# Linear attention and an ELU MLP on one core: a new start, 64x64 tiles for K^T V, a redistributed ELU and a new order around group 2

## The chip, the cores and the metric

The kernel runs on one core of a Trainium2 chip. The metric is the time of one execution on the device in microseconds (us). Each run also comes with its mean granted TensorE clock (1.0 is full speed).

Engine names: PE is TensorE's matmul, PEld its weight load, DVE VectorE, ACT ScalarE, POOL GpSimd, SP the queue that issues most stores and DMA transposes.

## The reference

```python
kv  = einsum('bhsd,bhse->bhde', k, v)            # per head: K^T V, 64 x 64
out = einsum('bhsd,bhde->bhse', q, kv)           # the "product"
x   = out / sqrt(mean(out*out, -1) + 1e-6) * g_norm
# heads side by side: x is [4608, 512]
h   = x @ w_in                                   # first layer, 512 -> 2048
g   = where(h > 0, h, exp(min(h, 0)) - 1)        # ELU
y   = g @ w_out                                  # second layer, 2048 -> 512
```

q, k and v are 8 batches x 8 heads x 576 rows x 64. The kernel works in nine groups of 512 tokens (512 rows of each batch; group 8 holds the 64 rows left over of each). A group needs 64 first-layer and 64 second-layer matmuls of 128x512, in bf16. While PE works on the MLP of group T, the attention of group T+1 is woven in.

## The kernel before

The start, for group 0: V lands, then twice, for each half of the heads, the same serial chain.

```python
def heads_half(u, se_ps, mean_ps, fill):
    kv_single(0, kv_ps, u)                       # K^T V, 36 matmuls of 64x64
    nc.vector.tensor_copy(out=kv0[:, u], in_=kv_ps[...])
    idle(fill[0])                                # idle matmuls
    ...                                          # product: 4 matmuls into se_ps
    for l in range(2): nc.scalar.activation(sq[l], se_ps[l], AF.Square)
    idle(fill[1])
    ...                                          # mean by a matmul
    for l in range(2):
        nc.scalar.activation(r[l], mean[:, l, :], AF.Ln, bias=eps_col)
        nc.scalar.activation(r[l], r[l], AF.Exp, scale=-0.5)
    for l in range(2): nc.vector.scalar_tensor_tensor(out=x0[...], ...)   # scale
heads_half(0, ..., (1, 3, 0)); heads_half(1, ..., (0, 0, 0))
```

K^T V of the groups from 2 on is computed two heads at a time, 128 wide (half of the result is thrown away), and the weights' side needs both heads side by side, so POOL first copies K into that layout:

```python
for j in range(9):
    for s in range(2):
        nc.tensor.matmul(kv_ps[s][:, u*128:u*128+128],
            lhsT=k_bf[rows, j, 2*u:2*u+2, :], rhs=v[rows, j, 2*u:2*u+2, :], ...)
def unpack(name, b, eng): ...                    # 3 copies of K, 4 of Q, on POOL
```

A "step" i of a group is 8 first-layer matmuls into one of two PSUM pairs, followed by the ELU: Exp on ACT, then min and subtract 1 (a tensor-scalar) and a max with the PSUM pair on DVE. In some steps (`relu`) ACT copies the positive part out of PSUM too, so that DVE no longer reads PSUM and has less work. The order around group 2:

```python
for i in range(2): elu(0, i, [(0, 2, firsts[i])], False)()
for i in range(2, 8): mm1(0, i, relu=i in (2, 4, 6), spare=i in (2, 5))()
...
# group 1; se0, se1: the two halves of group 2's product; x0, x1: its transposes
group(1, at, {"kv": 2, "se0": 4, "se1": 6}, {}, (1, 3, 5, 6), 1)
ahead["qd"]()                                    # DMA transpose of a later Q
mm2_quarter(1, 0, 0); mm2_quarter(1, 0, 1); at["x0"]()   # a quarter: 4 matmuls
mm2_quarter(1, 0, 2); at["x1"](); mm2_quarter(1, 0, 3)
```

The product's PSUM tile exists once: the next product or transpose can start only when DVE has scaled the rows of the one before.

## Time and profile before

| | before |
|---|---|
| time, median of 3 runs | 305.54 us (305.16 to 306.78) |
| span of the profiled run | 304.3 us |
| PE busy | 281.5 us (93%) |
| DVE, ACT, POOL busy | 56%, 47%, 21% |
| mean granted clock | 0.982 |

From the page of the kernel before: busy time by engine, then two rows of the view in 40 equal slices of 7.6 us (busy tenths of PE, tenths of the granted clock).

```profile
PE 281.5 (93%) x1760; PEld 136.1 (45%) x1789; DVE 170.1 (56%) x207; ACT 142.7 (47%) x201; POOL 63.9 (21%) x96
...
PE   7559989886698999999999999999999999999995
...
PEclk9769999999999999999999999999999999999999
```

PE is the bottleneck from slice 14 on, without gaps. In the first three slices it is a quarter to a half idle and its clock is down; slices 9 to 13 have gaps, the largest in 10 and 11. The windows view of the kernel before gives the same by stage. Columns: from:to, length, busy time and number of instructions of each engine, then clock, DMA share, GB/s.

```profile
0.00:25.19 25.19, 16.85 (x131) 6.96 (x134) 7.39 (x15) 10.98 (x17) 12.16 (x22) 0.80 1.07 190
25.19:37.82 12.63, 11.84 (x81) 5.43 (x80) 9.43 (x15) 10.89 (x15) 5.51 (x9) 1.00 1.24 206
37.82:51.81 13.99, 13.02 (x151) 7.22 (x153) 6.95 (x7) 6.14 (x11) 5.55 (x9) 1.00 1.27 188
51.81:83.38 31.57, 24.88 (x172) 12.84 (x173) 18.31 (x22) 18.59 (x26) 17.18 (x24) 1.00 1.20 172
83.38:110.97 27.59, 26.34 (x161) 12.75 (x164) 19.64 (x21) 13.34 (x19) 7.57 (x12) 1.00 0.88 140
110.97:304.30 193.33, 188.62 (x1071) 90.90 (x1087) 108.39 (x127) 82.80 (x116) 15.93 (x23) 1.00 0.41 86
```

The stages end with: group 0's first 16 first-layer matmuls; its other 48; the start of group 1's first layer; of group 2's; of group 3's. The start, in the PE timeline of the kernel before (start, length, what, count, idle time before and its releaser):

```profile
10.41 0.69 PE L191 MATMUL at<-v_pk,k_pk 64*64 64x64 bf16 x36 [2.02 <-DMA v_pk<-in_v_dram]
...
13.94 0.48 PE L191 MATMUL at<-v_pk,k_pk 64*64 64x64 bf16 x36
17.67 0.64 PE L559 MATMUL se_ps<-qT,kv 64*64 64x512 bf16 x4 [3.25 <-DVE kv L554]
...
20.29 5.07 PE L607 MATMUL h_ps<-xT,w_in_sb 128*128 128x512 bf16 x15 [0.22 <-issue]
```

The second half's K^T V is done at 14.4 us, but its product waits until 17.7 us for a copy that stands behind two scalings in DVE's queue. The 16 first matmuls take 4.9 us at the slow clock; at the fast one 16 take 3.45 us. The waits of PE between 51 and 111 us, in the waits view of the kernel before (total us, times, longest):

```profile
PE at L329 <- DVE xs L256: 2.4, 1, 2.4
PE h_ps L407 <- DVE gT L436: 2.1, 3, 0.7
PE at L222 <- DVE xs L256: 1.8, 2, 1.5
PE o_ps L452 <- ACT o_sb L462: 0.7, 1, 0.7
PE at L329 <- ACT xT L336: 0.3, 1, 0.3
```

Line 329 is the transpose of group 2's rows, 222 a product, 407 the first layer, 452 the second.

### The profile page before, as it was taken

Reading aid. Unit: us, or ns where it says so; the run is one execution under the profiler, and the core shown is the slowest. Engines: PE = TensorE matmul, PEld = TensorE weight load, DVE = VectorE, ACT = ScalarE, POOL = GpSimd, SP = SyncE. Lnnn points to the kernel's source line nnn. Section 1 sums busy time; section 2 is a strip of 40 time slices with the busy share of each in tenths; the row PEclk is TensorE's granted clock in tenths of the full one; section 3 lists DMA queues with packets and bytes.
Section 4 is the critical chain, followed back from the end, with each engine's and each line's share of the span. In section 5 each row is a group of like instructions: output and inputs, shape, how many; then the busy total and the mean of one; then the engine's idle time right before and its main releaser. Section 6 shows DMA issues by size and latency. Waiting matters only on the chain.

```text
span 304.3 us, 4381 instructions
## 1 busy us (share of the span) xinstructions
PE 281.5 (93%) x1760; PEld 136.1 (45%) x1789; DVE 170.1 (56%) x207; ACT 142.7 (47%) x201; POOL 63.9 (21%) x96
## 2 busy tenths in 40 slices
PE   7559989886698999999999999999999999999995
PEld 3213445443354445444544444454444444444444
DVE  5036745268539855765577547755774775554400
ACT  3466842578345544543553365345534554333311
POOL 8424309370944004500700000001100000000000
PEclk9769999999999999999999999999999999999999
DMA  7999999999799839696831313154715031101132
GB/s 180 184 206 203 206 203 189 177 214 155 118 182 125 176 88 150 80 175 117 133 103 34 105 35 104 37 124 107 151 34 139 2 103 34 71 0 69 50 91 69
DMA packets 56052, 35.94 MB, mean 118 GB/s; under 512 B 32864, under 2 KB 53600, under 8 KB 56032
## 3 DMA queue, kind: packets, MB, share of 16 engines
q0 software_dynamic: 20128, 17.30, 38.8%
q1 hardware_dynamic: 35504, 17.83, 26.7%
q10 hardware_dynamic: 400, 0.52, 0.5%
q8 instruction: 14, 0.23, 0.3%
q14 instruction: 6, 0.05, 0.1%
HBM read 36.70 MB, written 9.44 MB: 152 GB/s over the span
## 4 chain that ended last, share of the span: by engine, by line
PE 82%; DVE 8%; ACT 5%; DMA 3%; issue 2%; POOL 0%; DVEq 0%; POOLq 0%
PE h_ps L407 36%; PE o_ps L452 33%; PE o_ps L719 5%; DVE gT L436 3%; DMA v_pk<-in_v_dram 3%; ACT elu_e L419 2%; DVE elu_e L428 2%; PE at L177 2%; PE at L222 2%; PE h_ps L607 2%; DVE xs L256 1%; DVE ss L246 1%; PE at L329 1%; PE at L191 1%; DVE xT L338 1%
## 5 line engine op out<-in xcount | busy, mean ns | idle before, releaser
L407 PE MATMUL h_ps<-xT,w_in_sb 128*128 128x512 bf16 (+1 forms) x563 | 131.6, 376 | 3.4 <-DVE gT L436 2.9
L452 PE MATMUL o_ps<-w_out_sb,gT 128*128 128x512 bf16 x491 | 118.4, 379 | 1.8 <-ACT o_sb L462 0.7
L419 ACT ACTIVATE elu_e<-h_ps 128x1024 bf16<-128x1024 f32 (+1 forms) x74 | 73.8, 1004 | 90.9 <-PE h_ps L407 88.7
L407 PEld LDWEIGHTS <-w_in_sb 128*128 128x128 bf16 x568 | 54.2, 98 | 65.4 <-issue 4.8
L436 DVE TENSOR_TENSOR gT<-elu_e,h_ps 128x1024 bf16<-128x1024 bf16 (+1 forms) x66 | 79.5, 1205 | 6.9
L428 DVE TENSOR_SCALAR elu_e<-elu_e 128x1024 bf16<-128x1024 bf16 (+1 forms) x73 | 35.0, 479 | 76.1 <-ACT elu_e L419 75.8
L452 PEld LDWEIGHTS <-gT 128*128 128x128 bf16 x512 | 49.8, 98 | 60.0 <-issue 1.0
L462 ACT COPY o_sb<-o_ps 128x512 f32<-128x512 f32 x32 | 18.7, 586 | 20.8 <-PE o_ps L452 20.8
L246 DVE TENSOR_REDUCE ss<-sq 128x16 f32<-128x1024 bf16 x16 | 19.4, 1218 | 9.0 <-ACT sq L241 8.9
L152 POOL COPY q_bf<-q_pk 128x512 bf16<-128x512 bf16 x24 | 14.2, 637 | 25.2 <-DMA q_pk<-in_q_dram 13.0
L256 DVE TENSOR_TENSOR xs<-at,ss 128x1024 bf16<-128x1024 f32 x15 | 18.2, 1217 | 0.0
L121 POOL DMA_DIRECT2D v_pk<-in_v_dram x10 | 7.4, 740 | 48.0 <-PE at L177 44.9
L241 ACT ACTIVATE sq<-at 128x1024 bf16<-128x1024 f32 x15 | 15.4, 1026 | 3.5 <-PE at L222 3.5
L152 POOL CAST q_bf<-st_q 128x512 bf16<-128x512 f32 x4 | 2.6, 654 | 64.5 <-DMA st_q<-in_q_dram 64.5
L152 POOL COPY k_bf<-k_pk 128x768 bf16<-128x768 bf16 x18 | 15.1, 875 | 2.4 <-DMA k_pk<-in_k_dram 2.4
L719 PE MATMUL o_ps<-w_out_sb,gT 128*128 128x512 bf16 (+1 forms) x79 | 14.0, 336 | 0.1
L107 POOL DMA_DIRECT2D q_pk<-in_q_dram x14 | 10.4, 746 | 3.5 <-DMA v_pk<-in_v_dram 2.0
L719 PEld LDWEIGHTS <-gT 128*128 128x128 bf16 x80 | 7.8, 98 | 6.2
L222 PE MATMUL at<-bd_kv,qT 128*128 128x128 bf16 x104 | 7.9, 219 | 2.7 <-DVE xs L256 1.8
L222 PEld LDWEIGHTS <-qT 128*128 128x128 bf16 x112 | 7.3, 98 | 5.9 <-issue 3.1
L121 POOL DMA_DIRECT2D k_pk<-in_k_dram x10 | 7.5, 751 | 6.3 <-DMA w_in_sb<-in_moe_w_in_dram 2.8
L276 ACT CAST bd_kv<-at 64x256 bf16<-64x256 f32 x12 | 4.4, 367 | 8.3 <-PE at L177 8.2
(60 smaller groups left out, 113.0 us busy)
## 6 DMA issues: line engine op xcount, KB each, us to landing
out_dram<-o_sb SPq DMA_DIRECT2D x16, 512.0 KB, 2.9
q_pk<-in_q_dram POOLq DMA_DIRECT2D x14, 256.0 KB, 4.9
k_pk<-in_k_dram POOLq DMA_DIRECT2D x6, 576.0 KB, 9.8
v_pk<-in_v_dram POOLq DMA_DIRECT2D x6, 576.0 KB, 11.0
w_in_sb<-in_moe_w_in_dram POOLq DMA_DIRECT2D x4, 512.0 KB, 14.7
w_out_sb<-in_moe_w_out_dram POOLq DMA_DIRECT2D x4, 512.0 KB, 15.0
k_pk<-in_k_dram POOLq DMA_DIRECT2D x4, 288.0 KB, 11.7
v_pk<-in_v_dram POOLq DMA_DIRECT2D x4, 288.0 KB, 11.5
```

What stands on the lines that cost most here:

```text
L152: eng.tensor_copy(out=out_, in_=in_)
L222: nc.tensor.matmul(ov[:, u, :, s, :], lhsT=qT(p, j), rhs=bd_kv[:, T, p, :], start=True, stop=True,)
L241: nc.scalar.activation(sq, se_ps, AF.Square)
L246: nc.vector.reduce_sum(out=ss, in_=sq.rearrange("p c (h e) -> p (c h) e", h=H), axis=AX.X)
L256: nc.vector.tensor_tensor(out=xs.rearrange("p c (h e) -> p (c h) e", h=H), in0=se_ps.rearrange("p c (h e) -> p (c h) e", h=H), in1=ss.to_b ...
L407: nc.tensor.matmul(h_ps[a][:, cs], lhsT=w_in_sb[:, c, f * P : f * P + P], rhs=x(c, cs), start=(c == 0), stop=(c == KC - 1),)
L419: nc.scalar.activation(e[:, lo:hi, :], ps, AF.Exp)
L428: nc.vector.tensor_scalar(out=e[:, lo:hi, :], in0=e[:, lo:hi, :], scalar1=1.0, scalar2=1.0, op0=ALU.min, op1=ALU.subtract,)
L436: nc.vector.tensor_tensor(out=gT[T][:, 2 * i + lo : 2 * i + hi, :], in0=e[:, lo:hi, :], in1=h, op=ALU.add if relu else ALU.max,)
L452: nc.tensor.matmul(o_ps[T, j], lhsT=gT[T][:, f, j * P : j * P + P], rhs=w_out_sb[:, f, :], start=(f == 0), stop=(f == FC - 1),)
L462: nc.scalar.copy(o_sb[T][:, j % 2, :], o_ps.pop((T, j)))
L719: nc.tensor.matmul(ps, lhsT=gT[B][:, f, j * P : j * P + P], rhs=w_out_sb[:, f, cols], start=(f == 0), stop=(f == FC - 1),)
```

## The change

Its intent: shorten the start and keep the clock up, take work from PE (tiles) and POOL (K's copies), relieve DVE in group 0, and cover the waits before group 2 with second-layer matmuls of group 1. The core of the diff, with cuts marked:

```diff
# 1. start: halves interleaved, squares split, fillers on PE
-    heads_half(0, [...], lambda: idle_ps, (1, 3, 0))
-    heads_half(1, se_b, ..., (0, 0, 0))
+    kv_first(0); idle(idle_b, 1); se_first(0)
+    square_first(0, A); square_first(1, V)          # V: copy, then multiply
+    idle(idle_b, 3); mean_first(0); idle(idle_b, 1); mean_first(1)
+    log_first(0); exp_first(0); log_first(1)
+    kv_first(1); idle(idle_b, 1); se_first(1); scale_first(0)
+    square_first(2, A); exp_first(1); square_first(3, V); scale_first(1)
+    idle(..., 3); mean_first(2); log_first(2); exp_first(2); idle(..., 1)
+    mean_first(3); log_first(3); exp_first(3); scale_first(2); scale_first(3)
# 2. g_norm: two loads of 64 single numbers -> one row, turned by a matmul with [[1.0]]
# 3. ELU of group 0, and loads of w_out, q2, k2, v2 issued later (cut)
-    for i in range(2): elu(0, i, [(0, 2, firsts[i])], False)()
+    elu(0, 0, [(0, 2, firsts[0])], True, V)()
+    elu(0, 1, [(0, 2, firsts[1])], False, V)()
     for i in range(2, 8):
-        mm1(0, i, relu=i in (2, 4, 6), spare=i in (2, 5))()
+        mm1(0, i, relu=i in (2, 4, 6), spare=i in (2, 5), eng=Q if i in (3, 5) else V)()
# 4., 5. K^T V: kv_mm and K's unpack on POOL removed
+        def kv_all():
+            if T < B:
+                for u in range(2): kv_half(u)()     # 72 matmuls of 64x64
# 6. order around group 2
-    for j in (2, 3, 0, 1): mm2_quarter(0, j, 3)
+    for j in (2, 3): mm2_quarter(0, j, 3)
-    group(1, at, {"kv": 2, "se0": 4, "se1": 6}, {}, (1, 3, 5, 6), 1)
-    ahead["qd"](); ...                              # quarters between x0 and x1
+    ahead["qd"]()
+    second = {2: [(0, 0, 12, 16)], 3: [(0, 1, 12, 16)]}
+    group(1, at, {"kv": 2, "se0": 5, "se1": 7}, second, (1, 3, 5, 7), 1)
+    # and at its end: for j in range(2): mm2(T, j, 0, FC); at[f"x{j}"]()
-    group 2: 12 quarters of group 1's second layer, 1 and 2 per step in turn
+    group 2: 8 quarters, 1 per step
```

The numbers are those of the prediction's points.

More of the change, by code (lines that the diff above doesn't have):

```diff
@@ L123, in fetch_packed_kv, with unpack_q @@
         )
-    def unpack(name, b, eng):
-        t = raw.pop((name, b))
-        if name == "q":
-            bf["q", b] = qkvp.tile([P, J, H, D], BF16, name="q_bf", tag="q")
-            parts = [slice(j, j + 1) for j in range(J)]
-        else:
-            bf["k", b] = qkvp.tile([P, RK, 4, D], BF16, name="k_bf", tag="k")
-            parts = [slice(j, j + 3) for j in range(0, RK, 3)]
-        for js in parts:
-            copy_on(eng, bf[name, b][:, js].rearrange("p j h d -> p h j d"), t[:, :, js])
+    def unpack_q(b, eng):
+        t = raw.pop(("q", b))
+        bf["q", b] = qkvp.tile([P, J, H, D], BF16, name="q_bf", tag="q")
+        for j in range(J):
+            copy_on(eng, bf["q", b][:, j], t[:, :, j])
     def load_w_in(s):
@@ L170, in at_tile @@
         return full if dtype == FP32 else full.bitcast(BF16)
-    def kv_mm(T, kv_ps, u):
-        for j in range(RK):
-            for s in range(2):
-                rows = slice(s * 64, s * 64 + 64)
-                nc.tensor.matmul(
-                    kv_ps[s][:, u * P : u * P + P],
-                    lhsT=bf["k", T][rows, j, 2 * u : 2 * u + 2, :],
-                    rhs=bf["v", T][rows, j, 2 * u : 2 * u + 2, :],
-                    start=(j == 0),
-                    stop=(j == RK - 1),
-                )
     def kv_single(T, kv_ps, u):
@@ L264, in attention @@
         st = {}
-        def kv():
-            if T == B:
-                return
-            kv_ps = at_tile(FP32)
-            for u in range(2):
-                kv_mm(T, [kv_ps[:, 0:512], kv_ps[:, 512:1024]], u)
-            kv_v = kv_ps.rearrange("p (s x e) -> p s x e", s=2, e=P)[:, :, 0:2, :]
-            bd_v = bd_kv[:, T].rearrange("p (s u) e -> p s u e", s=2)
-            for l in range(2):
-                ls = slice(l * 64, l * 64 + 64)
-                nc.scalar.copy(bd_v[ls, :, :, ls], kv_v[ls, :, :, ls])
         def q_t():
@@ L359, in x_dma @@
             return turn, scale
+        def kv_all():
+            if T < B:
+                for u in range(2):
+                    kv_half(u)()
         def kv_half(u):
@@ L375, in kv_half @@
             return product
-        pieces = {"kv": kv, "q": q_t, "qd": q_dma}
+        pieces = {"kv": kv_all, "q": q_t, "qd": q_dma}
         for h in range(2):
@@ L389, with mm1 @@
     gT = {}
-    def mm1(T, i, cols=(slice(0, 512),), relu=False, spare=False):
+    def mm1(T, i, cols=(slice(0, 512),), relu=False, spare=False, eng=nc.vector):
         if i == 0:
@@ L413, in mm1, with elu @@
                     )
-        return elu(T, i, parts, relu)
-    def elu(T, i, parts, relu):
+        return elu(T, i, parts, relu, eng)
+    def elu(T, i, parts, relu, eng):
         e = mlpt.tile([P, 2, G], BF16, name="elu_e", tag="elu_e")
@@ L427, in rest @@
             for lo, hi, h in parts:
-                nc.vector.tensor_scalar(
+                eng.tensor_scalar(
                     out=e[:, lo:hi, :],
@@ L489 @@
     for u in range(2):
-        for name in "kv":
-            fetch_packed_kv(name, 0, slice(2 * u, 2 * u + 2))
-    make_identity(nc, ident)
+        fetch_packed_kv("k", 0, slice(2 * u, 2 * u + 2))
+        if u == 1:
+            make_identity(nc, ident)
+        fetch_packed_kv("v", 0, slice(2 * u, 2 * u + 2))
     for s in range(4):
@@ L496 @@
     packed_kv(1)
-    for u in range(2):
-        for name in "kv":
-            fetch_packed_kv(name, 1, slice(2 * u, 2 * u + 2))
-        load_w_out(u)
-    for s in range(2, 4):
-        load_w_out(s)
-    fetch_packed_q(2)
-    packed_kv(2)
     for name in "kv":
-        fetch_packed_kv(name, 2)
+        fetch_packed_kv(name, 1, slice(0, 2))
+    load_w_out(0)
+    for name in "kv":
+        fetch_packed_kv(name, 1, slice(2, 4))
     zeros = const.tile([P, 512], BF16, name="zeros")
@@ L513 @@
         nc.vector.memset(means[s * 64 : s * 64 + 64, s * 64 : s * 64 + 64], 1.0 / D)
+    one = const.tile([1, 1], FP32, name="one")
+    nc.vector.memset(one, 1.0)
     nc.vector.memset(bd_kv, 0.0)
     fetch_q(0)
-    g_src = bass.AP(tensor=g_norm.tensor, offset=g_norm.offset, ap=[[1, 64], [1, 1]])
-    for i in range(2):
-        nc.sync.dma_start(out=g_col[i * 64 : i * 64 + 64, :], in_=g_src)
+    g_row = const.tile([1, 2, D], FP32, name="g_row")
+    nc.sync.dma_start(
+        out=g_row,
+        in_=bass.AP(tensor=g_norm.tensor, offset=g_norm.offset, ap=[[1, 1], [0, 2], [1, 64]]),
+    )
     q_st = q_tile(0)
@@ L526, with idle @@
     ]
-    idle_ps = ps_m1.tile([P, 2, G], FP32, name="idle_ps", tag="mm1")
-    def idle(n):
+    def idle(ps, n):
         for _ in range(n):
-            nc.tensor.matmul(
-                idle_ps[:, 0, :], lhsT=zeros[:, 0:P], rhs=zeros, start=True, stop=True
-            )
-    idle(9)
+            nc.tensor.matmul(ps, lhsT=zeros[:, 0:P], rhs=zeros, start=True, stop=True)
+    idle_a = ps_m1.tile([P, 2, G], FP32, name="idle_ps", tag="mm1")
+    idle(idle_a[:, 0, :], 9)
     qT0 = attp.tile([P, NPAIR, G], BF16, name="qT", tag="qT")
@@ L543 @@
             nc.vector.tensor_copy(out=qT0[:, 0:2, :], in_=qt_ps[0])
-        idle(2)
+            idle(idle_a[:, 0, :], 2)
     nc.scalar.copy(qT0[:, 2:4, :], qt_ps[1])
+    nc.tensor.matmul(
+        idle_a[:, 1, 0:1],
+        lhsT=g_row.rearrange("p l d -> p (l d)"),
+        rhs=one,
+        start=True,
+        stop=True,
+    )
+    nc.vector.tensor_copy(out=g_col, in_=idle_a[:, 1, 0:1])
+    idle(idle_a[:, 0, :], 6)
     kv_ps = at_tile(FP32).rearrange("p (s x) -> p s x", s=2)
@@ L550, with kv_first, se_first @@
     xT[0] = lambda c, cs: x0[:, c, cs]
-    def heads_half(u, se_ps, mean_ps, fill):
+    sq0 = [attp.tile([P, G], BF16, name="sq0", tag="sq0", bufs=4) for _ in range(KC)]
+    r0 = [attp.tile([P, G], FP32, name="r0", tag="r0", bufs=4) for _ in range(KC)]
+    se0, mean0 = {}, {}
+    def kv_first(u):
         kv_single(0, kv_ps, u)
         nc.vector.tensor_copy(out=kv0[:, u], in_=kv_ps[:, :, u * 64 : u * 64 + 64])
-        idle(fill[0])
+    def se_first(u):
         for l in range(2):
@@ L559, in heads_half @@
                 nc.tensor.matmul(
-                    se_ps[l][s * 64 : s * 64 + 64, :],
+                    se0[2 * u + l][s * 64 : s * 64 + 64, :],
                     lhsT=kv0[ls, u, s, :],
@@ L565, in heads_half @@
                 )
-        sq, r = [], []
-        for l in range(2):
-            sq.append(attp.tile([P, G], BF16, name="sq0", tag="sq0", bufs=4))
-            nc.scalar.activation(sq[l], se_ps[l], AF.Square)
-        idle(fill[1])
-        mean = mean_ps()
-        for l in range(2):
-            nc.tensor.matmul(mean[:, l, :], lhsT=means, rhs=sq[l], start=True, stop=True)
-            if l == 0:
-                idle(fill[2])
-        for l in range(2):
-            r.append(attp.tile([P, G], FP32, name="r0", tag="r0", bufs=4))
-            nc.scalar.activation(r[l], mean[:, l, :], AF.Ln, bias=eps_col)
-            nc.scalar.activation(r[l], r[l], AF.Exp, scale=-0.5)
@@ L580, in heads_half @@
-        for l in range(2):
-            nc.vector.scalar_tensor_tensor(
-                out=x0[:, 2 * u + l, :],
-                in0=se_ps[l],
-                scalar=g_col,
-                in1=r[l],
-                op0=ALU.mult,
-                op1=ALU.mult,
-            )
-    se_a = ps_m1.tile([P, 2, G], FP32, name="se_ps", tag="mm1")
-    heads_half(0, [se_a[:, 0, :], se_a[:, 1, :]], lambda: idle_ps, (1, 3, 0))
-    se_b = [ps_m2.tile([P, DM], FP32, name="se_ps", tag="mm2") for _ in range(2)]
@@ L593, with square_first @@
-    heads_half(
-        1, se_b, lambda: at_tile(FP32).rearrange("p (c f) -> p c f", c=2), (0, 0, 0)
-    )
-    for l in range(2):
-        ls = slice(l * 64, l * 64 + 64)
-        nc.gpsimd.tensor_copy(
-            out=bd_kv[ls, 0].rearrange("p (s u) e -> p u s e", s=2)[:, :, :, ls], in_=kv0[ls]
-        )
+    def square_first(c, eng):
+        if eng is A:
+            nc.scalar.activation(sq0[c], se0[c], AF.Square)
+        else:
+            nc.vector.tensor_copy(out=r0[c], in_=se0[c])
+            nc.vector.tensor_tensor(out=sq0[c], in0=r0[c], in1=se0[c], op=ALU.mult)
@@ new lines, in mean_first, with log_first, exp_first, scale_first @@
+    def mean_first(c):
+        nc.tensor.matmul(mean0[c], lhsT=means, rhs=sq0[c], start=True, stop=True)
+    def log_first(c):
+        nc.scalar.activation(r0[c], mean0[c], AF.Ln, bias=eps_col)
+    def exp_first(c):
+        nc.scalar.activation(r0[c], r0[c], AF.Exp, scale=-0.5)
+    def scale_first(c):
+        nc.vector.scalar_tensor_tensor(
+            out=x0[:, c, :], in0=se0[c], scalar=g_col, in1=r0[c], op0=ALU.mult, op1=ALU.mult
+        )
+    mean_a = ps_m1.tile([P, 2, G], FP32, name="mean_ps", tag="mm1")
@@ new lines @@
+    se_a = ps_m1.tile([P, 2, G], FP32, name="se_ps", tag="mm1")
+    idle_b = ps_m2.tile([P, DM], FP32, name="idle_ps", tag="mm2")
+    for c in range(2):
+        se0[c], mean0[c] = se_a[:, c, :], mean_a[:, c, :]
+    kv_first(0)
+    idle(idle_b, 1)
+    se_first(0)
+    square_first(0, A)
+    square_first(1, V)
+    idle(idle_b, 3)
+    mean_first(0)
+    idle(idle_b, 1)
+    mean_first(1)
+    log_first(0)
+    exp_first(0)
+    log_first(1)
+    kv_first(1)
+    idle(idle_b, 1)
+    for c in range(2, 4):
+        se0[c] = ps_m2.tile([P, DM], FP32, name="se_ps", tag="mm2")
@@ new lines @@
+    se_first(1)
+    scale_first(0)
+    square_first(2, A)
+    exp_first(1)
+    square_first(3, V)
+    scale_first(1)
+    firsts = [ps_m1.tile([P, 2, G], FP32, name="h_ps", tag="mm1") for _ in range(2)]
+    mean_b = at_tile(FP32).rearrange("p (c f) -> p c f", c=2)
+    for c in range(2, 4):
+        mean0[c] = mean_b[:, c - 2, :]
+    idle(firsts[0][:, 0, :], 3)
+    mean_first(2)
+    log_first(2)
+    exp_first(2)
+    idle(firsts[0][:, 0, :], 1)
+    mean_first(3)
+    log_first(3)
+    exp_first(3)
@@ L602 @@
+    scale_first(2)
+    scale_first(3)
     gT[0] = mlpg.tile([P, FC, G], BF16, name="gT", tag="gT")
@@ L613 @@
                 )
-    for i in range(2):
-        elu(0, i, [(0, 2, firsts[i])], False)()
     at, ahead = attention(1), attention(2)
+    elu(0, 0, [(0, 2, firsts[0])], True, V)()
+    elu(0, 1, [(0, 2, firsts[1])], False, V)()
     for i in range(2, 8):
-        mm1(0, i, relu=i in (2, 4, 6), spare=i in (2, 5))()
+        mm1(0, i, relu=i in (2, 4, 6), spare=i in (2, 5), eng=Q if i in (3, 5) else V)()
+        if i == 2:
+            for l in range(2):
+                ls = slice(l * 64, l * 64 + 64)
+                nc.gpsimd.tensor_copy(
+                    out=bd_kv[ls, 0].rearrange("p (s u) e -> p u s e", s=2)[:, :, :, ls],
+                    in_=kv0[ls],
+                )
+        if i in (3, 5):
+            load_w_out(i // 2)
         if i == 5:
             at["q"]()
+    load_w_out(3)
+    fetch_packed_q(2)
+    packed_kv(2)
+    for name in "kv":
+        fetch_packed_kv(name, 2)
     at["kv0"]()
@@ L643 @@
     at["x1"]()
-    unpack("q", 2, Q)
-    unpack("k", 2, Q)
+    unpack_q(2, Q)
     ahead["qd"]()
     rest = mm1(1, 0, (slice(0, 256), slice(256, 512)))
-    for j in (2, 3, 0, 1):
+    for j in (2, 3):
         mm2_quarter(0, j, 3)
@@ L657, in fetch @@
                 fetch_packed_kv(name, b)
-            unpack("q", b, Q)
-            unpack("k", b, Q)
+            unpack_q(b, Q)
         else:
@@ L676, in group @@
                     at[name]()
+                for j in range(2):
+                    mm2(T, j, 0, FC)
+                    at[f"x{j}"]()
                 break
@@ L688 @@
     at, ahead = ahead, attention(3)
-    group(1, at, {"kv": 2, "se0": 4, "se1": 6}, {}, (1, 3, 5, 6), 1)
     ahead["qd"]()
-    mm2_quarter(1, 0, 0)
-    mm2_quarter(1, 0, 1)
-    at["x0"]()
-    mm2_quarter(1, 0, 2)
-    at["x1"]()
-    mm2_quarter(1, 0, 3)
+    second = {2: [(0, 0, 12, 16)], 3: [(0, 1, 12, 16)]}
+    group(1, at, {"kv": 2, "se0": 5, "se1": 7}, second, (1, 3, 5, 7), 1)
     for T in range(2, NT):
@@ L700 @@
         if T == 2:
-            quarters = [(1, j, 4 * i, 4 * i + 4) for j in range(1, J) for i in range(4)]
-            second = {i: [quarters.pop(0) for _ in range(1 + i % 2)] for i in range(8)}
+            second = {i: [(1, 2 + i // 4, 4 * (i % 4), 4 * (i % 4) + 4)] for i in range(8)}
         at, start = ahead, {}
```

## The prediction

> What bounds the kernel now. The page's busy table has PE at 93% of a 304.3 us span; the chain of waits is 82% PE. The timeline shows three stages. From group 3 on (110 us to the end) PE has no gaps: 8 matmuls of 128x512 start every 1.73 us, one group takes 29.7 us; only less PE work helps there. Groups 1 and 2 (52 to 111 us) have about 8 us of PE gaps: 0.7 us waits for the ELU on DVE, 1.5 us before group 2's second product, 2.4 us before its transposes, 0.7 and 0.3 us in group 2. The first 25 us are a serial chain (V lands at 10.4 us, then product, squares, mean, log, exp, scale, twice), with PE's clock slow: the first MLP matmuls (20.3 us) start 0.43 us apart until 23.7 us, then 0.216. That is the two-state gate of the Trainium skill, "TensorE: Matmul & The Clock Gate", Part 1; the trace agrees (ratio 2).
>
> What the change does.
>
> 1. Group 0: halves interleaved, squares split between ACT and DVE, fillers on PE. Now the second half's product waits (17.7 us) because its K^T V copy stands behind two scalings on DVE. I walked the new order through with the trace's durations (ACT square 0.59, log 0.68, exp 0.63, scale 0.75, product 0.64 us): the last scale ends near 20.6 us instead of 23.5. With the clock fast throughout, the 16 first matmuls end near 21.7 us, not 25.2. Gain 3.4 us, on the chain. I expect V's landing unmoved.
>
> 2. g_norm as one row: g_col lands 6 to 7 us after issue, before its first use at 15.4 us. Off the chain; 0 us.
>
> 3. Group 0's ELU: Relu on ACT frees the first PSUM pair about 0.7 us sooner but the second later; POOL's pass takes an estimated 1.2 us or more (its 128x768 copy takes 0.83). Net 0 to -0.5 us. Weight loads issued later keep their place in a backlogged queue (w_in lands up to 24.7 us).
>
> 4. K^T V in 64x64 tiles: now 36 matmuls take 1.11 us and the next eight 1.96 instead of 1.73. The tiled form in group 1 takes 0.41 us per half, with 0.1 us after it. Saving 0.4 us, six times, all on PE; 1.6 us of it in groups 3 to 6.
>
> 5. K's unpack leaves POOL (18 x 0.875 us). Its copies hold up DVE: one 128x1024 tensor-scalar took 2.97 instead of 0.43 us during them, before a 0.7 us PE gap. The skill's "SBUF — State Buffer" describes this exclusive shared port.
>
> 6. Group 2 led by product: 16 matmuls (3.45 us) run while sums and scale finish; the 2.4 us gap should shrink below 1 us. But its second product comes at step 7 and waits for the first scale: I estimate 2.6 us instead of 1.5. Group 2 gets 12 matmuls per step, enough for DVE's about 19 us against PE's 22.7. Groups 1 and 2 together: gain 3 to 4 us.
>
> Sum: 3.4 + 3.5 + 1.6 = 8.5, less about 0.3: near 297.3 us, 2.7% faster. Range 294.3 to 300.5. Chances: faster 0.80, same 0.18, slower 0.02.
>
> Signs: MLP's first matmuls 0.216 us apart, done by 22 us; group period 29.7 falls to 29.3; tensor-scalar maximum under 2 us in group 2.
>
> What would make it wrong: fillers that miss the clock's window (3 us lost); POOL's ELU slow or blocking DVE; V, w_out or the g row later; a longer wait before group 2's second product; DVE unable to keep up in group 2.

## The result

| | before | after |
|---|---|---|
| time, median of 4 runs | 305.44 us (305.16 to 306.78) | 301.33 us (300.92 to 302.34) |
| ratio, 95% interval | | 0.9862 (0.9824 to 0.990) |
| span of the profiled run | 304.3 us | 299.0 us |
| granted clock | 0.982 (profiled run) | 1.0 (profiled run), 0.994, 0.992, 0.992 |

A ratio here is the mean time of one kernel's runs over the mean of the other's in the same rounds, so it is not quite the ratio of the medians. Executions over 1.5% slower than the fastest of the same kernel are left out of the means. The change brought 1.4%, about half of the forecast 2.7%, and fell outside the range. From the page of the changed kernel, the rows shown of before:

```profile
PE 280.5 (94%) x2017; PEld 134.3 (45%) x2017; DVE 168.6 (56%) x210; ACT 142.7 (48%) x200; POOL 56.5 (19%) x81
...
PE   7888789896888999999999999999999999999995
...
PEclk9999999999999999999999999999999999999999
```

And the same stages in the windows view of the changed kernel:

```profile
0.00:21.29 21.29, 16.70 (x146) 7.28 (x146) 10.22 (x21) 9.78 (x15) 11.75 (x21) 1.00 1.07 203
21.29:35.48 14.19, 11.82 (x83) 5.51 (x81) 7.06 (x11) 11.86 (x16) 9.28 (x8) 1.00 1.23 192
35.48:49.47 13.99, 13.13 (x154) 7.20 (x153) 8.02 (x9) 6.06 (x11) 5.36 (x8) 1.00 1.11 166
49.47:83.21 33.74, 27.92 (x228) 14.17 (x226) 17.50 (x22) 19.76 (x27) 13.02 (x21) 1.00 1.21 191
83.21:106.59 23.38, 22.58 (x184) 10.73 (x183) 17.13 (x20) 12.03 (x17) 5.40 (x8) 1.00 0.74 125
106.59:299.00 192.41, 188.31 (x1233) 89.45 (x1232) 108.64 (x128) 83.22 (x117) 11.66 (x18) 1.00 0.42 90
```

Subtracting stage by stage:

| stage | before | after | gain | forecast |
|---|---|---|---|---|
| start, to the end of the first 16 matmuls | 25.19 | 21.29 | 3.90 | 3.4 |
| rest of group 0's first layer | 12.63 | 14.19 | -1.56 | 0 to -0.5 |
| to group 1's first layer | 13.99 | 13.99 | 0 | 0 |
| groups 1 and 2 (16 second-layer matmuls moved from 2 to 1, so only the sum compares) | 59.16 | 57.12 | 2.04 | 3 to 4 |
| from group 3 on | 193.33 | 192.41 | 0.92 | 1.6 |
| sum | 304.3 | 299.0 | 5.3 | 8.2 |

The medians differ by 4.1 us only, because the profiled runs are not the middle ones: before's took 306.07 us, 0.6 above its median, and the changed kernel's 300.92 us, its fastest, 0.4 below.

**The start** went nearly as forecast, in the PE timeline of the changed kernel:

```profile
9.99 0.48 PE L173 MATMUL at<-v_pk,k_pk 64*64 64x64 bf16 x36
...
14.63 0.41 PE L545 MATMUL se_ps<-qT,kv 64*64 64x512 bf16 x4
...
17.84 3.61 PE L621 MATMUL h_ps<-xT,w_in_sb 128*128 128x512 bf16 x16
21.29 3.65 PE L382 MATMUL h_ps<-xT,w_in_sb 128*128 128x512 bf16 x16
25.75 3.61 PE L382 MATMUL h_ps<-xT,w_in_sb 128*128 128x512 bf16 x16 [0.81 <-DVE gT L411]
...
31.93 3.61 PE L382 MATMUL h_ps<-xT,w_in_sb 128*128 128x512 bf16 x16 [1.55 <-DVE gT L411]
```

The second product runs at 14.6 instead of 17.7 us and the first 16 matmuls take 3.45 us. PE no longer waits for V: the fillers ahead of it end at 9.9 us and V is there by then, whereas before PE waited for it until 10.4 us. Which of the small changes to the first loads did that was not tried. K^T V so starts 0.4 us sooner, which is 0.4 of the 3.9 us and was not forecast; the rest, 3.5, is close to the 3.4.

**The loss in group 0** shows in the last line: 1.55 us. It waits for DVE's max, and DVE waited for POOL. POOL's timeline in the changed kernel, between 22 and 34 us:

```profile
26.98 3.65 POOL L403 TENSOR_SCALAR elu_e<-elu_e 128x1024 bf16<-128x1024 bf16 x1 [4.82 <-ACT elu_e L394]
...
31.45 3.82 POOL L403 TENSOR_SCALAR elu_e<-elu_e 128x512 bf16<-128x512 bf16 x2
```

DVE does the same pass over 128x1024 in 0.43 us. I had scaled POOL's plain copy (0.83 us for 128x768) to "1.2 us or more". DVE ran nothing between 26.8 and 30.7 us, so the 3.65 us are not a contest between the two engines.

**Groups 1 and 2.** PE's waits between 49 and 110 us, in the waits view of the changed kernel:

```profile
PE at L204 <- DVE xs L238: 3.1, 2, 2.3
PE h_ps L382 <- DVE gT L411: 1.0, 2, 0.7
PE h_ps L382 <- DVE xT L308: 0.9, 1, 0.9
PE o_ps L427 <- ACT o_sb L437: 0.8, 1, 0.8
PE at L299 <- DVE xs L238: 0.8, 1, 0.8
```

Line 204 is the product, 299 the transpose. The wait before the transposes fell from 2.4 to 0.8 us, but the one before the second product grew from 1.5 to 2.3, a new one of 0.9 us stands before group 2's first layer (its second transpose is now the last thing before it), and 0.8 us before a product inside group 2 (before had 0.3 there, and 0.7 for an ELU).

**From group 3 on** the period of a group is 29.3 us (139.83 to 169.16 us, from K^T V to K^T V), against 29.7 before, as forecast. But two groups have a new wait; the PE timeline of the changed kernel has one of them:

```profile
110.15 0.78 PE L173 MATMUL at<-v_pk,k_pk 64*64 64x64 bf16 x72
110.86 1.90 PE L382 MATMUL h_ps<-xT,w_in_sb 128*128 128x512 bf16 x8
112.60 1.89 PE L427 MATMUL o_ps<-w_out_sb,gT 128*128 128x512 bf16 x8
114.66 0.62 PE L204 MATMUL at<-bd_kv,qT 128*128 128x128 bf16 x8 [0.17 <-DMA qT<-q_bf]
```

PE, now sooner at the product, waits for the DMA transpose of Q.

### The profile page after: what moved, and what is told of

Read it like the earlier page. It is cut to its first block, busy times and chain, and to the rows that moved or that the text cites. A ratio compares the mean times of both kernels' runs of the same rounds, so it can differ in the third digit from the quotient of the medians.

```text
span 299.0 us, 4843 instructions
## 1 busy us (share of the span) xinstructions
PE 280.5 (94%) x2017; PEld 134.3 (45%) x2017; DVE 168.6 (56%) x210; ACT 142.7 (48%) x200; POOL 56.5 (19%) x81
## 4 chain that ended last, share of the span: by engine, by line
PE 79%; DVE 7%; ACT 6%; DMA 5%; POOL 1%; issue 1%; SPq 0%; DVEq 0%; ACTq 0%; POOLq 0%
PE h_ps L382 34%; PE o_ps L427 32%; PE o_ps L741 5%; DMA qT<-q_bf 5%; ACT elu_e L394 2%; DVE gT L411 2%; PE at L204 2%; PE idle_ps L505 2%; PE at L173 1%; POOL elu_e L403 1%; DVE ss L228 1%; DVE xs L238 1%; PE h_ps L621 1%; ACT elu_h L398 1%; DVE elu_e L403 1%
## 5 line engine op out<-in xcount | busy, mean ns | idle before, releaser
L427 PE MATMUL o_ps<-w_out_sb,gT 128*128 128x512 bf16 x512 | 121.1, 379 | 0.8 <-ACT o_sb L437 0.8
L411 DVE TENSOR_TENSOR gT<-elu_e,h_ps 128x1024 bf16<-128x1024 bf16 (+1 forms) x65 | 78.3, 1205 | 11.7 <-POOL elu_e L403 5.3
L403 DVE TENSOR_SCALAR elu_e<-elu_e 128x1024 bf16<-128x1024 bf16 x70 | 31.4, 448 | 72.3 <-ACT elu_e L394 72.3
L107 POOL DMA_DIRECT2D q_pk<-in_q_dram x14 | 10.4, 752 | 0.7 <-DMA v_pk<-in_v_dram 0.7
L345 ACT CAST bd_kv<-at 64x256 bf16<-64x256 f32 x14 | 5.1, 367 | 9.7 <-PE at L173 9.6
L505 PE MATMUL idle_ps<-zeros 128*128 128x512 bf16 x23 | 8.1, 480 | 1.5 <-DVE zeros L480 1.2
L403 POOL TENSOR_SCALAR elu_e<-elu_e 128x512 bf16<-128x512 bf16 (+1 forms) x3 | 7.5, 2501 | 4.9 <-ACT elu_e L394 4.8
(64 smaller groups left out, 111.3 us busy)
## 6 DMA issues: line engine op xcount, KB each, us to landing
v_pk<-in_v_dram POOLq DMA_DIRECT2D x4, 288.0 KB, 10.4
```

The lines of the kernel that those rows point to most:

```text
L403: eng.tensor_scalar(out=e[:, lo:hi, :], in0=e[:, lo:hi, :], scalar1=1.0, scalar2=1.0, op0=ALU.min, op1=ALU.subtract,)
L411: nc.vector.tensor_tensor(out=gT[T][:, 2 * i + lo : 2 * i + hi, :], in0=e[:, lo:hi, :], in1=h, op=ALU.add if relu else ALU.max,)
L427: nc.tensor.matmul(o_ps[T, j], lhsT=gT[T][:, f, j * P : j * P + P], rhs=w_out_sb[:, f, :], start=(f == 0), stop=(f == FC - 1),)
```

## The experiments

All gave correct results. Edits are to the changed kernel ("after") unless said. For differences between two edits I take the ratios times 305.5 us, which removes most of the difference between chips. The changed kernel itself was not run again: its 0.9862 is from its own rounds, and 0.4% (1.2 us) is the half width of its interval, so single differences under about 1 us are not resolved by times alone.

| run | what | median us | ratio to before (95%) |
|---|---|---|---|
| after | the change | 301.33 | 0.9862 (0.9824 to 0.9900) |
| e1_dve_elu | without POOL's ELU passes | 299.83 | 0.9809 (0.9780 to 0.9838) |
| e2_old_order | order around group 2 undone | 301.21 | 0.9842 (0.9813 to 0.9870) |
| e3_old_kv | K^T V and K's unpack undone | 304.00 | 0.9944 (0.9906 to 0.9981) |
| e6_tiles_unpack | only K's unpack back | 302.77 | 0.9885 (0.9849 to 0.9922) |
| e4_no_fill | without fillers after V | 305.02 | 0.9989 (0.9947 to 1.0030) |
| e5_start_only | before + the new start | 302.66 | 0.9898 (0.9869 to 0.9927) |
| e7_qd_early | Q's transpose issued earlier | 300.70 | 0.9828 (0.9799 to 0.9856) |
| e8_lead | product at step 4, x1 inside the second layer | 299.14 | 0.9785 (0.9754 to 0.9816) |
| e9_best | e1 + e7 + order with 24 matmuls ahead | 295.11 | 0.9645 (0.9630 to 0.9661) |
| e10_best_fewfill | e9 with fewer fillers ahead of V | 295.36 | 0.9657 (0.9627 to 0.9688) |
| e11_fill_gap | idle matmuls in the 2.3 us gap | 302.06 | 0.9869 (0.9849 to 0.9890) |
| e12_kv_only | before + tiles, no unpack | 302.75 | 0.9887 (0.9868 to 0.9907) |
| e13_best_again | e9 again | 295.21 | 0.9645 (0.9616 to 0.9674) |
| e14_lead24 | order with 24 matmuls ahead, nothing else | 298.40 | 0.9735 (0.9707 to 0.9764) |
| e15_order_only | before + the new order | 307.37 | 1.0038 (1.0010 to 1.0066) |

### POOL's share of the ELU

```diff
-        mm1(0, i, ..., eng=Q if i in (3, 5) else V)()
+        mm1(0, i, ..., eng=V)()
```

> The changed kernel (301.3 us) with the two POOL passes of group 0's ELU given back to DVE, nothing else. Theory A: POOL's pass of 3.65 us holds a PSUM pair and caused the 1.55 us PE gap; the stretch from the end of the first 16 matmuls to group 1's K^T V (14.2 us after, 12.6 before) falls to about 12.9, the time by about 1.3 us, to 300.0. Rival: DVE needed the relief; the gap only moves to DVE's own queue, the stretch stays at 13.8 or more, the time at 301 to 302.

Median 299.83 us; by ratios 1.6 us under the changed kernel. In its trace group 1's K^T V starts at 33.89 us instead of 35.48, and the 1.55 us gap is gone; the 0.82 us one remains. DVE did not need the relief. Theory A holds.

### The order around group 2, undone

The edit restores the lines of point 6 of the diff, and nothing else.

> The changed kernel with the order of groups 1 and 2 as before (products at steps 4 and 6, transposes led by single quarters, three quarters of group 1's second layer in group 2). Theory A: the new order brought the 1.3 us gained in group 1 and most of the 0.8 us of group 2: undoing it costs about 2 us, 303.3. Rival: the 2.3 us wait it put before group 2's second product eats the gain and group 2 gained because K's unpack left POOL: undoing it costs less than 0.7 us, 301 to 302.

Median 301.21 us, ratio 0.9842: undoing it costs nothing. The rival holds. PE's waits between 49 and 110 us, in the waits view of this kernel:

```profile
PE at L299 <- DVE xs L238: 2.3, 1, 2.3
PE at L204 <- DVE xs L238: 1.5, 1, 1.5
PE h_ps L382 <- DVE gT L411: 1.2, 2, 0.8
PE o_ps L427 <- ACT o_sb L437: 0.8, 1, 0.8
```

They sum to 5.8 us against 6.6 in the changed kernel. The old order has no waits in group 2 at all once K^T V is short and K's unpack is gone: its odd steps hold 16 matmuls, the new order's only 12 (as a cause this is argued, not tested).

### K^T V and K's unpack

e3 restores both; e6 keeps the tiles but lets POOL copy K first, as before. (The fourth combination, the 128-wide form on the packed K, was not run.)

```diff
 e6, after each unpack of Q:
+    unpack_k(b, Q)            # 3 copies of 128x768; the tiles read k_bf
 e3, besides:
-    for u in range(2): kv_half(u)()
+    for u in range(2): kv_mm(T, ..., u)     # 36 matmuls, 128 wide
```

> The changed kernel with K^T V 128 wide from an unpacked K again (36 matmuls, POOL's 18 copies). Theory A: 0.41 us per group comes back six times, the two qT waits (0.5 us) vanish: about +2 us, 303.3; group period 29.7. Theory B (POOL's copies also block DVE in groups 1 and 2): +3 us, 304.3, with a tensor-scalar over 2 us there.

> The changed kernel with the 64x64 tiles, but reading a K that POOL unpacks first (the 18 copies are back, the matmuls are not). Parts the two effects of e3. Theory A: POOL is off the path, time within 0.3 us of 301.3. Theory B: its copies hold DVE up in groups 1 and 2: +0.7 to +1.5 us, with a tensor-scalar over 2 us.

e3: 304.00 us, by ratios 2.5 us over the changed kernel. It lies between the two theories; the tensor-scalar over 2 us that B asked for is absent (longest 0.97). Of this, e3 minus e6 is 1.8 us by ratios (1.2 by medians): PE's part. The rest, 0.7 (1.4 by medians), is the unpack's; e6's runs scatter from 301.0 to 304.5 and its interval overlaps that of the changed kernel, so this size is not settled. What a copy on POOL can do is seen in the traces, and in these two it is not what I had said. In e6 no tensor-scalar reached 2 us (longest 0.99), and DVE's 16 between 49 and 112 us took 543 ns on the mean against 467. The larger effect is on a DMA. The chain of waits of e6 between 95 and 112 us:

```profile
97.62 9.80 DMA xT<-xs
...
107.45 0.48 DVE xT L334
...
110.05 1.90 PE h_ps L389 x8
```

The DMA transpose of x took 9.8 us from issue to landing, where the slower of the changed kernel's two took 4.2 in this stretch, and PE stood 1.5 us before group 3 (e3: 1.4 us; the changed kernel: none). With the unpack, K's buffer comes free when POOL has copied it, and POOL issued K's next load at 97.2 us, beside the transposes; without it, K is held until K^T V has read it, and the same load is issued at 111.3 us. That the two transfers collide is my reading of these times; it was not tested alone. The other traces go with it: the slower of these two transposes took 9.7 and 9.8 us in e3 and e6, where K's load was issued 0.4 to 0.5 us ahead of the first, 5.4 to 8.0 where it was issued 4.2 us ahead (before, e5, e15), and 4.2 to 6.9 in the ten traces of kernels without the unpack. PE waited for it in e3 and e6 only, so this is not what the unpack cost in the kernel before.

```diff
 e12, from the kernel before:
-        pieces = {"kv": kv, ...}
+        pieces = {"kv": kv_all, ...}        # 64x64 tiles
-    unpack("k", 2, Q)
-            unpack("k", b, Q)
```

> The kernel before with only the 64x64 tiles of K^T V and no unpack of K. Theory A: the parts add up: 2.2 to 3.2 us under before (ratio 0.990 to 0.993), as undoing it in the changed kernel cost 2.7 us, about half by PE and half because POOL's copies no longer block DVE. Rival: it only helps behind the new order of groups 1 and 2: under 1.2 us here, ratio above 0.996.

302.75 us, ratio 0.9887: 3.1 us (medians) to 3.5 us (ratio) under before. Theory A holds, and the part is worth at least as much alone as in the change. Here POOL's copies did hold DVE up: before, e5 and e15 each have one tensor-scalar of 2.97 to 2.98 us beside K's copies in group 2, followed by PE waits of 0.7 and 0.3 us in before and e5; in e12 the longest is 0.94 us, and PE waits for nothing in group 2. These 1.0 us with the forecast 2.4 of point 4 make 3.4.

### The start and its fillers

```diff
 e4: every idle(...) between kv_first(0) and the first-layer matmuls removed
-    idle(idle_b, 1)
-    idle(idle_b, 3)
     ...
 e5: the changed kernel with points 3 to 6 undone
```

> The changed kernel without the ten filler matmuls between V's landing and the MLP's first matmul. Theory A: they keep the clock up; without them the mean granted clock of the profiled run falls below 0.99 and the 16 first matmuls start 0.43 us apart for some or all of their length: +2 to +3.4 us, 303.3 to 304.7. Rival: the shorter chain alone brings the start's 3.9 us, the fillers nothing: within 0.5 us of the changed kernel.

> The kernel before with the new start alone (interleaved halves, fillers, g row); ELU, K^T V, order and loads as before. Theory A: the parts add up, and the start brings 3.9 us by itself: 3 to 4 us under before, ratio 0.987 to 0.990. Rival: the groups behind it swallow a part of the shift (loads or POOL arrive no sooner): under 2 us, ratio above 0.993.

e4: 305.02 us, 3.7 us over the changed kernel, slightly more than theory A said. In its trace the first 16 matmuls start at 18.49 us and last until 23.33 (4.8 us instead of 3.45), and the granted clock of the profiled run is 0.981. So the idle matmuls, which compute nothing, are worth 2.0 us of the start's 3.9. The other half of e4's loss stands elsewhere in its trace: PE waits 2.3 us before group 2's first product for Q's DMA transpose (18.4 us from issue to landing, 10.8 in the changed kernel), and a stretch at half clock follows. Whether these come of the missing fillers or of chance is open. e5: 3.1 us under before, ratio 0.9898, within theory A: nothing behind the start swallows it. In its profiled run (clock 0.989) the clock fell inside the start, at 16 to 20 us, and the first 16 matmuls ended at 22.37 us instead of 21.29; its three runs at 0.999 or more took 301.7 to 302.4 us, 3.4 to 4.1 under before.

### Q's DMA transpose

```diff
-        group(T, at, start, second)
-        ahead["qd"]()
+        group(T, at, start, second, turn=ahead["qd"])   # called at the end of step 6
```

> The changed kernel with the DMA transpose of Q issued in step 6 of a group instead of behind the group's last store. Theory A: since K^T V became shorter, PE reaches the product before qT has landed; issued earlier, both waits on qT (0.17 and 0.33 us in the profile) vanish: -0.3 to -0.9 us. Rival: the transpose is late because of its data or of DMA load: the waits stay, 0 us.

300.70 us, by ratios 1.0 us under the changed kernel (0.6 by medians). Both waits on qT are gone from its trace. This agrees with theory A, at the edge of what the runs resolve.

### The order's idea, cut differently

```diff
-    group(1, at, {"kv": 2, "se0": 5, "se1": 7}, ...)
+    group(1, at, {"kv": 2, "se0": 4, "se1": 7}, ...)
 e8:   16 of mm2; x0; 8 of mm2; x1; 8 of mm2      (after: 16; x0; 16; x1)
 e14:  24 of mm2; x0; 4 of mm2; x1; 4 of mm2
 e9, e13: as e14, with the edits of e1 and e7
 e10:  as e9, and idle(..., 2) instead of idle(..., 6) ahead of V
```

> The changed kernel with group 2's first product at step 4 instead of 5, and its second transpose in the middle of the 16 matmuls instead of after them. Theory A: the 2.3 us wait before the second product and the 0.9 us before group 2 are made by that order alone; both shrink below 0.5 us: -2 to -3 us, 298.3 to 299.3. Rival: group 1 is bound by ACT and DVE, the wait moves to the ELU's PSUM pairs: less than 1 us.

299.14 us, 2.2 us under the changed kernel. The waits before the second product and before group 2 are gone, but one of 2.1 us stands before the first transpose: 16 matmuls (3.45 us) are too few to cover square, sums, root and scale of the second product, which in that trace end 6.1 us after the product began. Theory A had the time and its two waits right, and missed the one that came in their place.

> The changed kernel with product 0 of group 2 at step 4 and 24 of the 32 second-layer matmuls ahead of the first transpose; POOL's ELU and the late Q transpose stay. Theory A: the idea of the order was sound but short by one step and eight matmuls: -3.5 to -4.5 us, 296.8 to 297.8, the waits before second product, transposes and group 2 all below 0.7 us. Rival: e9 gained from the ELU and the Q transpose mostly: less than 2.5 us here, above 298.8.

Ratio 0.9735, 3.9 us under the changed kernel; four runs between 297.4 and 298.9 us. Theory A holds: the idea was sound, and one step and eight matmuls short. A fifth run (302.32 us at 0.987) counts as slow and is left out. Its profiled execution was a slow outlier of 408.7 us at a granted clock of 0.684, so its waits were not read.

> The changed kernel with the repairs together: ELU of group 0 on DVE (-1.5 us by e1), Q's transpose earlier (-0.4), product at step 4 (e8), and 24 of the 32 second-layer matmuls before group 2's first transpose, so that the scale is done when PE gets there. Theory A: the repairs lie in different stretches and add up: 295 to 296.5 us, no PE gap over 1 us between 50 and 84 us, granted clock 0.998 or more in nearly all runs. Rival: a wait appears behind each one removed: 297.5 or more.

> The kernel of e9 again, unchanged. Theory A: 294.8 to 295.6 us, as four of its five runs; the 1036 us belonged to that execution, not to the kernel. Rival: the long execution comes back in one run of five. The profile should show no PE gap over 1 us between 50 and 84 us and no slow clock there.

> The same with 2 instead of 6 fillers ahead of V's landing, which in the changed kernel ended 0.7 us after V could be used (9.9 against about 9.26 us). Theory A: -0.4 to -0.7 us. Rival: the clock falls before the product, and the time grows by up to 3 us in some runs.

e9: 295.11 us, with four runs between 294.8 and 295.2 and one of 1036 us; e13, the same kernel, 295.21 us in five runs without an outlier. The ratio is 0.9645 both times, 3.6% faster than before, and 2.2% under the changed kernel by ratios. The repairs add up. PE's waits between 47 and 104 us, in the waits view of e13:

```profile
PE h_ps L382 <- DVE gT L411: 1.0, 2, 0.7
PE at L204 <- DVE xs L238: 0.8, 1, 0.8
PE o_ps L427 <- ACT o_sb L437: 0.7, 1, 0.7
PE at L299 <- DVE xs L238: 0.4, 1, 0.4
PE at L299 <- ACT xT L306: 0.3, 1, 0.3
```

3.2 us in place of 6.6. Fewer fillers ahead of V (e10) made no difference that the runs resolve; its six runs scatter over 3.3 us, e13's five over 1.5. In its trace the start did end 1.0 us sooner (20.29 us, V being there by 9.0), and its two fastest runs, 293.9 and 294.1 us, are below all of e9 and e13; the others lost it again, one at a clock of 0.992, the rest for no reason found.

> The kernel before with only the new order of groups 1 and 2 (K^T V wide, K unpacked on POOL). Theory A: the order moves waits and brings nothing by itself: within 0.8 us of before, ratio 0.997 to 1.003. Rival: it brings the 2 to 2.5 us I forecast when POOL's copies are still in the way, and the other changes make it redundant: ratio 0.991 to 0.994.

307.37 us, ratio 1.0038 (1.0010 to 1.0066): the order alone makes the kernel before slower, by about 1.2 us. Theory A expected nothing; the rival's gain is excluded. Its trace shows the 2.3 us wait before the second product, and in group 2, which has fewer second-layer matmuls per step, waits of 1.6 and 1.2 us where before had 0.7 and 0.3, behind the same tensor-scalar of 2.98 us. With K's copies still on POOL, the new order makes that hold-up dearer.

### The clock in the middle of the kernel

In several profiled runs the granted clock fell to one half once more, after one of the waits before group 2. From the PE timeline of e7:

```profile
72.87 1.01 PE L204 MATMUL at<-bd_kv,qT 128*128 128x128 bf16 x8 [2.52 <-DVE xs L238]
73.68 4.92 PE L427 MATMUL o_ps<-w_out_sb,gT 128*128 128x512 bf16 x16
78.43 0.61 PE L299 MATMUL at<-ident,xs 128*128 128x128 bf16 x8
```

From the first of the 16 matmuls to what follows are 4.75 us, not 3.45: 1.3 us lost, and the eight matmuls before them take nearly twice as long (0.81 us instead of 0.45). Read in windows of 2 us, seven of the profiled runs (e2, e4, e5, e6, e7, e8, e15) have one such stretch, each after a wait of 2.1 to 2.7 us; five others with a wait of that length (before, after, e1, e3, e12) have none there; e10 and e13, without the wait, have none. That goes with the scatter of single runs: e8's were 298.2 to 298.6 us at a clock of 1.0, and 299.7 to 300.3 at 0.994. One window at half clock lowers the mean by about 0.006 (an estimate: 3.4 us of half clock in 300, with the window's length from the Trainium skill, "TensorE: Matmul & The Clock Gate", Part 1, which says that it runs freely and does not start with the kernel; the traces here agree: each of the seven stretches, added up over its windows, is 3.4 us at 0.5). The changed kernel's runs, at 1.0, 0.994, 0.992 and 0.992, would by this estimate have had none, one, and one to two such windows; the last three were not traced.

```diff
             rest = mm1(T, i, ...)
+            if T == 1 and i == 7: idle(<a free PSUM bank>, 9)
```

> The changed kernel with nine idle matmuls (1.9 us) in the 2.3 us PE gap before group 2's second product. They do no useful work. Theory A: in most runs of the changed kernel that gap lets the granted clock fall (three of four runs at 0.992 to 0.994, the profiled one at 1.0), and the matmuls after it run slow for about 1 us or more: with fillers nearly all runs are at 0.998 or more and the median falls by 0.5 to 1.3 us although PE does more. Rival: the low clocks come from the start: runs stay mixed, median 301 or more.

302.06 us; clocks 0.993, 1.0, 0.992, 1.0, 0.992. Theory A fails: filling the gap with idle matmuls neither kept the clock up in most runs nor saved time. In its profiled run the slow stretch was at 16 to 20 us, in the start, where the interleaved chain still has PE gaps of 0.6 to 0.9 us. So the clock can fall in either place (in e5's profiled run it fell in both). Which of them cost the changed kernel's slower runs, and why e9 and e13, with the same start, ran at 0.998 or more in eight of nine fast runs, stays open.

## Why the prediction was wrong

The parts, each measured alone or undone, against the forecast:

| point | forecast | measured |
|---|---|---|
| 1, 2: start | -3.4 | -3.1 (e5); -3.9 in the profiled run |
| 3: ELU with POOL | 0 to +0.5 | +1.6 (e1) |
| 4, 5: K^T V, unpack | -2.4 for point 4; point 5 not sized apart | -2.5 (e3), -3.1 to -3.5 (e12) |
| 6: order | about -2.7 with point 5 (below) | 0 to +0.6 (e2), +1.2 (e15) |
| sum | -8.5 + 0.3 | -3.4 to -5.0 |

The forecast of 3 to 4 us for groups 1 and 2 included 0.8 us of point 4; the middle of it, less that, leaves 2.7 for the order and for what point 5 brings there (1.0 by e12's trace), so about 1.7 for the order alone. The sum of the measured column lies between -3.4 and -5.0 with e5, e1, e3 or e12, and e2 (-3.1 + 1.6 - 2.5 + 0.6 at one end, -3.1 + 1.6 - 3.5 + 0 at the other); the change measured -4.1. The parts add up as far as the runs resolve, so the error lies in the terms.

- **The step that failed is the sixth: "16 matmuls (3.45 us) run while sums and scale finish; the 2.4 us gap should shrink below 1 us", "Groups 1 and 2 together: gain 3 to 4 us".** The gap did shrink, to 0.8 us, and the wait before the second product did grow, to 2.3 us against my 2.6. What I did not do is add up both sides: 1.6 us less in one wait, 0.8 more in another, 0.9 before group 2, and group 2 robbed of four matmuls in each of four steps, so that DVE shows again (0.8 us in the changed kernel, none in e2; 2.7 in e15, beside K's copies). I also compared my walk through the new order with the old order *as it stood in the profile of before*, where short K^T V and the missing unpack were not yet in. The waits shown for these groups sum to 7.3 us in before, to 5.8 in e2, which has the other changes but the old order, and to 6.6 in the changed kernel. e2 is the right comparison, and it shows none of the gain belonging to the order; e15 shows none against before either. e14 shows that the idea was worth 3.9 us over the order as I had cut it, with 24 matmuls ahead and the product one step earlier.
- **In the third point "POOL's pass takes an estimated 1.2 us or more" was mis-sized:** 3.65 us. A plain copy's rate does not carry over to a two-operation pass. I had the place (a PSUM pair held longer) and the sign; e1 shows 1.6 us instead of at most 0.5.
- **"With the clock fast throughout"** was right for the profiled run and not for the median one. e4 shows that the fillers are needed; the runs' clocks show that they are not always enough. By the times this is about 0.4 us (the median run against the profiled one); the larger part of the step from 5.3 us in the profiles to 4.1 in the medians is that before's profiled run was 0.6 us slower than its median.
- **The start's 3.4 us (point 1)** was right in its chain; the 0.5 us more in the profile is mostly luck, as V came sooner than the 10.4 us that I held fixed.
- **The fourth point, 0.4 us per group**, was right in the period (29.7 to 29.3 us), but 0.5 us of waits for Q's transpose came in its place where PE got ahead of it; e7 removes them.
- **The fifth point's mechanism was right for the kernel before, and not the only one.** I expected DVE to be held up on the port it shares with POOL, which the Trainium skill, "SBUF — State Buffer", section "Who interferes with whom", describes. The traces agree as far as they go: the pass of 2.97 us in before comes again in e5 and e15, beside the same copies, and is gone in e12 with its two waits. In e3 and e6, where the copies run a little later, DVE's passes are only somewhat slower (543 against 467 ns in e6), and the wait that ends last is a DMA transpose.

## What to carry to other kernels

Judge a new order against the old one with all the other changes already in, and sum every wait that it moves, not only the one that it was made for; matmuls used to cover a wait are missing where they came from. Before giving an engine work that it has not done in the profile, find a duration of that very operation; a copy's rate is no measure for a two-operation pass. When PE gets shorter, look at what it will now reach too early: here a DMA transpose that had just been in time.

## What the Trainium skill lacked or had wrong

- "GPSIMD Engine Reference", section 4.1, calls one-input elementwise work on GpSimd roughly line-rate, and section 8 puts the Vector engine at about twice as fast. A tensor-scalar of two operations (min, subtract) on 128x1024 bf16 took 3.65 us on POOL and 0.43 us on DVE, 8.5 times (128x512: 1.92 us), though POOL's copy of 128x768 took 0.83 us. DVE was idle during the long pass, so no contention explains POOL's 3.6 ns per column.
- "TensorE: Matmul & The Clock Gate", the table "Why this matters for your kernels", warns of PE gaps over about 3 us. Here gaps of 2.1 to 2.7 us were followed by a stretch at half clock in seven of twelve profiled runs, each lengthening the matmuls in it by 1.5 to 1.7 us.
- The same page, "Back-to-back issue gap", gives a floor of about 25 ns from matmul to matmul. In 64x64 tiles 72 matmuls took 0.71 us from the first to the start of what followed, 9.9 ns each. That is no contradiction: the page's Part 3 has tiles at different positions start about 4 ns apart. What it lacks is a figure for a long stream of 64x64 tiles.
- The same page calls the clock binary and mentions one stuck at a quarter for 50 us and more. e14's first execution, 408.7 us, fits neither: the granted clock is 0.65 to 0.75 in windows of 50 us throughout, and 0.65 in twelve windows of 0.5 us from 100 us on, so it is not half and full clock in turn, as in the stretches of 3.4 us above. e9's first, 1036 us, is near the quarter in pace, but to its end: 16 matmuls of 128x512 took 13.1 us (0.82 us each, 3.8 times the usual) while the granted clock read 1.0. Both were first executions of a kernel, the ones profiled; what caused them was not found, and e13 did not repeat it.
- No page has a size for how much longer a DMA transpose takes when a POOL-issued load is issued just ahead of it: 9.7 and 9.8 us in e3 and e6, against 4.2 to 6.9 in ten traces without that load. It was read from traces, not isolated.
